# Linear attention feeding a gated MLP: an earlier load of v for batch 4, and another place for relu and minimum of phi(q) in one output stage

## Chip, cores and metric

The kernel runs on one core of a Trainium2 chip. The metric is device time of one launch, in microseconds (us). Of three runs of the kernel before, the median is 271.7 us (271.31 to 272.31).

## What is computed

The reference, cut to what matters (B = 8 batches, 8 heads, S = 576 tokens, head size 64):

```python
phi = lambda x: np.where(x > 0, x, np.exp(x) - 1.0) + 1.0
q_p, k_p = phi(q), phi(k)
kv  = einsum('bhsd,bhse->bhde', k_p, v);  z = sum(k_p, axis=2)
x   = einsum('bhsd,bhde->bhse', q_p, kv) / (einsum('bhsd,bhd->bhs', q_p, z) + 1e-6)
x   = x.transpose(0, 2, 1, 3).reshape(4608, 512)
h   = x @ w_in                          # 512 -> 2048
out = (h * sigmoid(beta * h)) @ w_out   # 2048 -> 512, float32
```

phi(x) is computed as min(exp(x), max(x, 0) + 1): an exponential on ScalarE (ACT, tile `e`, L169), "relu", that is max(x, 0) + 1, on VectorE (DVE, tile `r`, L176), and the minimum of both on VectorE (tile `phi_q` or `phi_k`, L182). Each is done in two halves of the heads (`pr` 0 and 1).

## The kernel before, in words

The order of every engine's queue is written out by hand; semaphores for the dependences are put in by the framework. The work runs in blocks b = 0 to 8. Block b is the MLP for 512 tokens of batch b (the 64 "odd" tokens of each batch that are left over are kept in `xT_tail` and make up block 8). A block has two stages. The H stage computes h = x @ w_in and the gate into `g` (for b = 1 in `h_phase`, for later blocks in `h_fast`, where part of the products is saved by sums and differences of blocks of x and w). The Y stage, `y_fast`, computes the product with w_out by seven products of half size.

In Y the order on TensorE (PE) is: `ya`, `yd` with the sums 2, `ya` again, `yc`, `yb`, then `yd` again with g and `yb` again. Between them VectorE computes u2 = yc + r1 (L1118) and u3 = yd + u2 (L1119), then y2's right half from yb and u3 (L1128), y2's left half from the second yd and u2 (L1131), and y1's right half from the second yb and u2 (L1139). The second `yd` accumulates into the same PSUM bank that u3 reads, so it waits for u3.

Attention for later batches is woven into these stages through two tables, `sh` for H and `sy` for Y: `at(sy, 3, f)` appends f to the list that `run(side, 3)` calls at that place of the stage (L1111 to L1149 show the places of Y: place 2 stands ahead of `yc` and the u sums, place 3 behind them, place 4 behind y2's right half). While block b is computed, batch n = b + 1 has its kv product (`kv_both`, L231, reading `phi_k` and `vaug`) and its numerator (`numer_all`, L344, reading the transposed `qTd`), and batch m = b + 2 has its phi(q) and phi(k). phi(q) is transposed by two DMAs of the SP queue (`q_trans_dma`, L281) into `qTd`.

v of a batch is loaded as float32 into the one tile `vf` (`load_v`, L99, a DMA from the POOL queue) and cast from there to `vaug` (`v_copy`): for batch 3 by ScalarE at place 0 of Y of block 1 (L247), for batches 4 to 7 by GpSimd (POOL, L249) in `next_cast` at place 7 of H. `next_cast` first runs a small copy (`gate`, L1163) that reads what VectorE last wrote, so that the cast starts late enough. Likewise `next_loads(b)` runs a small copy (`gate`, L1156) that reads the end of `qTd` of batch b, so that the loads of v, q and k behind it in the POOL queue start only when the transposes of phi(q) have landed. `tail_copy` (L379) copies the odd tokens of a batch out of `xT` into `xT_tail`, on POOL.

After the H stage's numerator, VectorE forms sums and differences of `g` in `stage` (L831 the differences, L835 to L837 the sums; all bf16, two inputs in SBUF) for the Y stage.

Of the kernel before, what the change touches and what calls it, by code (L numbers as in the profile page):

```python
# [16 lines left out]
def kernel(  # L17
# [12 lines left out]
    B, H, S, D = q.shape  # L30
# [67 lines left out]
    def load(eng, dst, src, b, i0=0, n=4):  # L98
        return eng.dma_start(  # L99
            out=dst.rearrange("p i j d -> p i (j d)"),  # L100
            in_=src[b].rearrange("(i a) (g j) d -> (a g) i (j d)", a=2, j=J)[:, i0 : i0 + n],
        )
# [58 lines left out]
    def table(func):  # L161
        nc.scalar.activation(act0, ones, func)  # L162
# [4 lines left out]
    def phi_exp(b, a, pr, x):  # L167
        e = work.tile([P, 2, J, D], BF16, tag="e", name="e", bufs=4)
        nc.scalar.activation(e, x, ACTF.Exp)  # L169
        st[b, a, pr, "e"] = e  # L170

    def phi_relu(b, a, pr, x):
        if pr == 0:
            st[b, a, "r"] = work.tile([P, 2, 2, J, D], BF16, tag="r", name="r")
        r = st[b, a, pr, "r"] = st[b, a, "r"][:, pr]
        nc.vector.tensor_scalar(r, x, 0.0, 1.0, ALU.max, ALU.add)  # L176

    def phi_tile(b, a):
        st[b, a] = work.tile([P, 2, J, P], BF16, tag=f"phi{a}", name=f"phi_{a}", bufs=1)

    def phi_min(b, a, pr):
        nc.vector.tensor_tensor(  # L182
            st[b, a][:, pr].rearrange("p j (h d) -> p j h d", h=2),
            st[b, a, pr, "e"].rearrange("p h j d -> p j h d"),
            st[b, a, pr, "r"].rearrange("p h j d -> p j h d"),
            ALU.min,
        )

    def xin(b, a, pr):
        if b == 0:  # L190
            return x0f[pr if a == "q" else 2 + pr]
        return (xk if a == "k" else xq)[b % 2][:, 2 * pr : 2 * pr + 2]

    def phi_part(b, a, pr):
        x = xin(b, a, pr)
        phi_exp(b, a, pr, x)
        phi_relu(b, a, pr, x)
        phi_min(b, a, pr)
# [11 lines left out]
    def v_copy(eng, b, pr):  # L210

        copy(
            eng, vaug[b % 2][:, pr, :, :, 0:D],
            (v0b if b == 1 else vf)[:, 2 * pr : 2 * pr + 2].rearrange("p h j d -> p j h d"),
        )
# [5 lines left out]
    def kv_both(b):  # L221

        t = banks("kvp")
        for pr in range(2):
            for j in range(J):
                for il in range(2):
                    for a in range(2):  # L230
                        nc.tensor.matmul(  # L231
                            t[half(il), a, pr * EA : (pr + 1) * EA],
                            st[b, "k"][half(a), pr, j, il * D : (il + 1) * D],
                            vaug[b % 2][half(a), pr, j, il, 0:EA],
                            start=(j == 0), stop=(j == J - 1), skip_group_check=True,
                        )
        tv = t[:, :, 0 : 2 * EA].rearrange("p a (r e) -> p a r e", r=2)
        if b > 1:
            nc.vector.tensor_copy(kv_q[b % 2], tv)
            return  # L240
        st[b, "kv"] = kv_bd.rearrange("p a r h e -> p a r (h e)")
        for il in range(2):
            copy((nc.scalar, nc.vector)[il], kv_bd[half(il), :, :, il], tv[half(il)])
# [34 lines left out]
    def q_trans_dma(b):  # L278
        st[b, "qTd"] = work.tile([P, 2, 2 * J, G], BF16, tag="qT", name="qTd", bufs=1)
        for hh in range(2):  # L280
            nc.sync.dma_start_transpose(  # L281
                out=st[b, "qTd"][:, hh],
                in_=st[b, "q"][half(hh)].rearrange("p a j c -> p (a j c)"),
            )
# [93 lines left out]
    def tail_copy(b):  # L378
        nc.gpsimd.tensor_copy(  # L379
            xT_tail[:, :, b].rearrange("p i r n -> p i (r n)"), xT[b % 2][:, :, 8]  # L380
        )
# [17 lines left out]
    def x_trans_dma(b, t=NT - 1):  # L399
        for pr in range(2):  # L400
            nc.sync.dma_start_transpose(
                out=xT_tail[:, :, b, pr],
                in_=st[b, "xs", t][: rows_of(t), pr * HM : (pr + 1) * HM],
            )
# [64 lines left out]
    def load_qk(b):  # L469
        if b < B:  # L470
            load(nc.gpsimd, xq[b % 2], q, b)
            load(nc.gpsimd, xk[b % 2], k, b)

    def load_v(b):
        if b < B:
            load(nc.gpsimd, v0b if b == 1 else vf, v, b)
# [4 lines left out]
    def w_sum(k, ns=range(2)):  # L481

        for n in ns:
            r = slice(4 * n, 4 * n + 4)
            a, b = (
                (wq(n, HM), wq(n, 0)),
                (wq(2 + n, HM), ws[0][:, r]),
                (wq(2 + n, HM), wq(n, HM)),
                (wq(2 + n, 0), ws[1][:, r]),
            )[k]  # L490
            nc.vector.tensor_sub(ws[k][:, r], a, b)
# [334 lines left out]
    def at(side, n, *fs):  # L826
        side.setdefault(n, []).extend(fs)
# [54 lines left out]
    def h_x_sums(b):  # L882

        t = [h_xs[:, k] for k in range(4)]
        x = lambda r, t: h_x_plain(b, r, t)

        def like(a, c):
            return a.rearrange("p i (t n) -> p i t n", n=c.shape[-1])

        for k, (u, w) in enumerate((  # L890
            (x(0, 1), x(0, 0)), (x(1, 1), t[0]), (x(1, 1), x(0, 1)), (x(1, 0), t[1])
        )):
            nc.vector.tensor_sub(like(t[k], u), u, like(w, u) if k % 2 else w)
# [257 lines left out]
    def next_loads(b):  # L1151

        for pr in range(2) if b == 2 else ():
            v_copy(nc.gpsimd, b, pr)
        if b + 1 < B:
            nc.gpsimd.tensor_copy(gate, st[b, "qTd"][:, 1, 2 * J - 1, G - 1 : G])  # L1156
            load_v(b + 1)
            if b > 2:
                load_qk(b + 1)

    def next_cast(b):

        nc.gpsimd.tensor_copy(gate, gs[2][:, 7, HM - 1 : HM])  # L1163
        for pr in range(2):
            v_copy(nc.gpsimd, b + 1, pr)

    for b in range(1, B + 1):
        n, m = b + 1, b + 2
        sh, sy = {}, {}
        if b == 2 or b == B - 1:  # L1170
            at(sh, 0, lambda: tail_copy(b))
        if n < B:
            at(sh, 0, lambda: next_loads(n))
            if b > 1 and n + 1 < B:
                at(sh, 7, lambda: next_cast(n))
            if b > 2:
                at(sh, 7, lambda: tail_copy(b))
            at(sh, 9 if b == 1 else 0, lambda: kv_both(n))
            at(sh, 12 if b == 1 else 10, lambda: numer_all(n))
        if b == 1:  # L1180
            at(sh, 4, lambda: w_sum(2))
            at(sh, 9, lambda: w_sum(1))
            at(sy, 0, lambda: w_sum(3))
        if m < B:
            at(sy, 0, lambda: phi_tile(m, "q"), lambda: phi_tile(m, "k"))
            if b == 1:

                for pr in range(2):
                    at(sy, 0, lambda pr=pr: phi_exp(m, "q", pr, xin(m, "q", pr)))
                    at(sy, 2, lambda pr=pr: phi_relu(m, "q", pr, xin(m, "q", pr)))  # L1190
                    at(sy, 3 + pr, lambda pr=pr: phi_min(m, "q", pr))
                for pr in range(2):
                    at(sy, 0, lambda pr=pr: v_copy(nc.scalar, m, pr))
                at(sy, 4, lambda: q_trans_dma(m))
                for pr in range(2):
                    at(sy, 5, lambda pr=pr: phi_exp(m, "k", pr, xin(m, "k", pr)))
                    at(sy, 5, lambda pr=pr: phi_relu(m, "k", pr, xin(m, "k", pr)))
                at(sy, 6, lambda: h_x_sums(n))
                for pr in range(2):
                    at(sy, 6, lambda pr=pr: phi_min(m, "k", pr))  # L1200
                at(sy, 6, lambda: table(ACTF.Silu), lambda: x_trans_dma(1, NT - 1))
            else:
                at(sy, 0, lambda: phi_part(m, "q", 0))
                at(sy, 1, lambda: phi_part(m, "q", 1))
                at(sy, 1, lambda: q_trans_dma(m))
                at(sy, 4, lambda: phi_part(m, "k", 0))
                at(sy, 4, lambda: phi_part(m, "k", 1), lambda: table(ACTF.Silu))
        if b == B - 2:
            at(sy, 0, lambda: h_w_sums(2))
        if 2 <= b < B:  # L1210
            at(sy, {B - 2: 4, B - 1: 0}.get(b, 6), lambda: h_x_sums(n))
        (h_phase if b < 2 else h_fast)(b, xT[b % 2] if b < B else xT_tail, sh)
        y_fast(b, sy)
# [30 lines left out]
```

## Time and profile before

| what | value |
|---|---|
| median of three runs | 271.7 us |
| the profiled execution, its own time | 271.53 us |
| span of its instructions | 269.8 us |
| PE busy in the span | 262.0 us (97%) |
| DVE busy | 211.3 us (78%) |
| ACT busy | 169.0 us (63%) |
| POOL busy | 46.0 us (17%) |
| TensorE clock granted | 1.0 |

Times below are microseconds from the start of the span. In a timeline a row has the start, the time from the start to the end of the merged instructions, the engine, the line, the operation, what it writes and reads, the count, and in brackets how long the engine had been idle and on what. Starts of successive PE rows tell more than their ends, which overlap: two products of 16 matmuls stand 1.75 us apart when PE does not wait. Y of block 1 runs from 64.77 to about 77.3, H of block 2 to 92.5, Y of block 2 from 92.53 to about 105.7.

### The profile page before, as it was taken

The page shows a single profiled execution, that of the slowest core. Times are in us where ns is not written, and L with a number is a line of the kernel's source. Part 1 is how long each engine was busy: PE and PEld are TensorE (multiplying, and loading weights), DVE is VectorE, ACT ScalarE, POOL GpSimd, SP SyncE. Part 2 cuts the span into 40 slices and gives each one's busy share as a digit, 9 for nine tenths or more (in the row PEclk, how much of TensorE's full clock was granted, in tenths as well). Part 3 has the DMA queues.
Part 4 walks back from the last instruction along what each step waited for, and adds up shares of the span by engine and source line. Part 5 has one row for each costly group of instructions (what it writes and reads, how often), then busy time and mean ns, then how long its engine had stood idle before and what let it go on. Part 6 is the DMA issues. An engine that isn't in the chain of part 4 may idle for free.

```text
span 269.8 us, 6793 instructions
## 1 busy us (share of the span) xinstructions
PE 262.0 (97%) x2846; PEld 182.1 (68%) x2851; DVE 211.3 (78%) x412; ACT 169.0 (63%) x241; POOL 46.0 (17%) x72
## 2 busy tenths in 40 slices
PE   7899999999999998999999999999999999999994
PEld 3584455446866586658864886588658866886793
DVE  4853697998995999689968986899689667856862
ACT  4958885987954993499449944894483048415810
POOL 5842305121003300340034003300000000000000
PEclk9999999999999999999999999999999999999999
DMA  7999999999349997998599979995504050023013
GB/s 235 242 206 286 303 326 239 299 212 260 74 78 229 245 145 104 277 217 90 90 255 243 99 92 248 242 108 87 158 2 88 4 156 2 0 64 94 0 41 117
DMA packets 49262, 42.19 MB, mean 156 GB/s; under 512 B 30400, under 2 KB 41296, under 8 KB 49232
## 3 DMA queue, kind: packets, MB, share of 16 engines
q0 software_dynamic: 13344, 22.81, 37.6%
q1 hardware_dynamic: 35568, 18.75, 35.4%
q8 instruction: 22, 0.36, 0.5%
q10 hardware_dynamic: 320, 0.20, 0.3%
q14 instruction: 8, 0.07, 0.1%
HBM read 36.71 MB, written 9.44 MB: 171 GB/s over the span
## 4 chain that ended last, share of the span: by engine, by line
PE 61%; DVE 1%; issue 0%; DVEq 0%
PE h_ps L413 21%; PE yd L1095 8%; PE ya L1095 8%; PE yb L1095 7%; PE hc L902 5%; PE hz L902 4%; PE yc L1095 4%; PE yb L1067 1%; PE kvp L231 1%; PE nps L344 1%; DVE phi_q L182 1%; DVE u L1119 0%; DVE u L1118 0%; DVE r L176 0%; DVE y L1075 0%
## 5 line engine op out<-in xcount | busy, mean ns | idle before, releaser
L421 ACT ACTIVATE g<-h_ps,beta_c 128x512 bf16<-128x512 f32 x108 | 71.5, 692 | 60.7 <-PE h_ps L413 60.1
L413 PE MATMUL h_ps<-xT,w_in 128*128 128x512 bf16 (+2 forms) x424 | 94.8, 367 | 0.0
L413 PEld LDWEIGHTS <-w_in 128*128 128x128 bf16 x456 | 42.8, 98 | 37.9
L1095 PEld LDWEIGHTS <-stage 128*128 128x128 bf16 x480 | 46.9, 98 | 5.6 <-DVE stage L831 0.2
L1095 PEld LDWEIGHTS <-g 128*128 128x128 bf16 x384 | 37.5, 98 | 7.2 <-issue 1.2
L1095 PE MATMUL ya<-w_out,g 128*128 128x256 bf16 x256 | 30.6, 273 | 0.0
L359 DVE TENSOR_TENSOR xs_sb<-nps,rden 128x448 bf16<-128x448 f32 (+2 forms) x24 | 18.2, 758 | 0.8
L169 ACT ACTIVATE e<-xk 128x1152 bf16<-128x1152 bf16 (+1 forms) x15 | 16.7, 1159 | 0.4 <-DMA xk<-in_k_dram 0.4
L1095 PE MATMUL yd<-ws,g 128*128 128x256 bf16 x128 | 15.3, 272 | 0.9 <-DVE u L1119 0.9
L962 ACT ACTIVATE g<-hc,beta_c 128x512 bf16<-128x512 f32 x18 | 11.4, 683 | 7.3 <-DVE hc L948 7.3
L169 ACT ACTIVATE e<-xq 128x1152 bf16<-128x1152 bf16 x14 | 15.6, 1159 | 0.0
L162 ACT ACT_TABLE_LOAD x12 | 15.4, 1283 | 0.2
L1095 PE MATMUL yd<-ws,stage 128*128 128x256 bf16 x128 | 15.3, 273 | 0.0
L1095 PE MATMUL yc<-ws,stage 128*128 128x256 bf16 x128 | 15.3, 273 | 0.0
L428 PE MATMUL y_ps<-w_out,g 128*128 128x512 bf16 x60 | 14.8, 379 | 0.2
L182 DVE TENSOR_TENSOR phi_q<-e,r 128x1152 bf16<-128x1152 bf16 x16 | 12.3, 767 | 2.2 <-ACT e L169 1.2
L902 PEld LDWEIGHTS <-w_in 128*128 128x128 bf16 x108 | 10.5, 98 | 4.9
L182 DVE TENSOR_TENSOR phi_k<-e,r 128x1152 bf16<-128x1152 bf16 x16 | 12.7, 803 | 1.2
L902 PEld LDWEIGHTS <-h_w 128*128 128x128 bf16 x112 | 11.0, 98 | 3.8
L1095 PE MATMUL yb<-ws,stage 128*128 128x256 bf16 x112 | 13.4, 273 | 0.0
L1095 PE MATMUL yb<-w_out,stage 128*128 128x256 bf16 x112 | 13.4, 273 | 0.0
L962 ACT ACTIVATE g<-c,beta_c 128x512 bf16<-128x512 f32 x18 | 12.3, 727 | 0.9 <-DVE c L945 0.9
(146 smaller groups left out, 375.3 us busy)
## 6 DMA issues: line engine op xcount, KB each, us to landing
out_dram<-y SPq DMA_DIRECT2D x29, 256.0 KB, 3.8
vf<-in_v_dram POOLq DMA_DIRECT2D x6, 1152.0 KB, 9.3
xq<-in_q_dram POOLq DMA_DIRECT2D x7, 576.0 KB, 13.6
xk<-in_k_dram POOLq DMA_DIRECT2D x7, 576.0 KB, 15.7
g<-in_moe_w_out_dram POOLq DMA_DIRECT2D x2, 1024.0 KB, 17.7
stage<-in_moe_w_out_dram POOLq DMA_DIRECT2D x4, 512.0 KB, 17.6
w_in<-in_moe_w_in_dram POOLq DMA_DIRECT2D x3, 512.0 KB, 12.7
stage<-in_q_dram SPq DMA_DIRECT2D x2, 576.0 KB, 4.4
```

The source lines that it names most:

```text
L162: nc.scalar.activation(act0, ones, func)
L169: nc.scalar.activation(e, x, ACTF.Exp)
L182: nc.vector.tensor_tensor(st[b, a][:, pr].rearrange("p j (h d) -> p j h d", h=2), st[b, a, pr, "e"].rearrange("p h j d -> p j h d"), st[b, ...
L231: nc.tensor.matmul(t[half(il), a, pr * EA : (pr + 1) * EA], st[b, "k"][half(a), pr, j, il * D : (il + 1) * D], vaug[b % 2][half(a), pr, j, ...
L344: nc.tensor.matmul(ps[half(n), v % 7 * EA : (v % 7 + 1) * EA], st[b, "qTd"][half(il), a, pr * J + j, :], kv_q[b % 2][half(il), a, pr, :], ...
L359: nc.vector.tensor_mul(xs_sb[:, ils, v0 * D : v1 * D].rearrange("p i (u d) -> p i u d", d=D), pv[:, :, :, 0:D], rden[:, :, :, None].to_bro ...
L413: nc.tensor.matmul(hp[:, c0:c1].rearrange("p (t n) -> p t n", n=n), w_in_sb[ff // 4][:, kc, (ff % 4) * P : (ff % 4 + 1) * P], xm, start=(f ...
L421: nc.scalar.activation(g_sb[b % 2][:, ff, :], hp, ACTF.Silu, scale=beta_c[:, ff : ff + 1])
L428: nc.tensor.matmul(yp[:, c0:c1], g_sb[b % 2][:, ff, t * P : (t + 1) * P], w_out_sb[i][:, c, c0:c1], start=(ff == 0), stop=(ff == FC - 1), ...
L902: nc.tensor.matmul(o, lhs[:, i, a * P : (a + 1) * P], m, start=(first and a == 0 and i == 0), stop=True, skip_group_check=True,)
L962: nc.scalar.activation(g_sb[b % 2][:, ff].rearrange("p (t n) -> p t n", t=2), src, ACTF.Silu, scale=beta_c[:, ff : ff + 1],)
L1095: nc.tensor.matmul(ps[:, p * HM : (p + 1) * HM], lhs(c, p), rhs(c), start=(first and p == 0 and c == 0), stop=True, skip_group_check=True,)
```

## The change

In H of block 2 (`next_loads(3)`) the load of v of batch 4 is put ahead of the gate on `qTd` of batch 3; q and k of batch 4 stay behind it. `tail_copy(2)` is put behind these loads; it stood ahead of all of them. So POOL's order there goes from tail copy, gate, v, q, k to v, gate, q, k, tail copy.

In Y of block 1 both relus of q (batch 3) go from place 2 to place 3, and the minimum of half 0 from place 3 to place 4, where that of half 1 stood. So DVE's order there goes from relu, relu, u2, u3, min, y2 right, min, y2 left to u2, u3, relu, relu, y2 right, min, min, y2 left. The two transposes of phi(q) stay behind the second minimum.

```diff
@@ next_loads(b)
         if b + 1 < B:
+            if b == 3:
+                load_v(b + 1)
             nc.gpsimd.tensor_copy(gate, st[b, "qTd"][:, 1, 2 * J - 1, G - 1 : G])
-            load_v(b + 1)
+            if b != 3:
+                load_v(b + 1)
             if b > 2:
                 load_qk(b + 1)
@@ the loop over blocks
-        if b == 2 or b == B - 1:
+        if b == B - 1:
             at(sh, 0, lambda: tail_copy(b))
         if n < B:
             at(sh, 0, lambda: next_loads(n))
+            if b == 2:
+                at(sh, 0, lambda: tail_copy(b))
...
                 for pr in range(2):
                     at(sy, 0, lambda pr=pr: phi_exp(m, "q", pr, xin(m, "q", pr)))
-                    at(sy, 2, lambda pr=pr: phi_relu(m, "q", pr, xin(m, "q", pr)))
-                    at(sy, 3 + pr, lambda pr=pr: phi_min(m, "q", pr))
+                    at(sy, 3, lambda pr=pr: phi_relu(m, "q", pr, xin(m, "q", pr)))
+                    at(sy, 4, lambda pr=pr: phi_min(m, "q", pr))
```

## The prediction

> **What bounds the kernel now.** I read the engines' shares first, then the chain of waits in order of time, then the timelines of PE, DVE and POOL around its start.
>
> ```profile
> PE 262.0 (97%) x2846; PEld 182.1 (68%) x2851; DVE 211.3 (78%) x412; ACT 169.0 (63%) x241; POOL 46.0 (17%) x72
> ```
>
> PE is busy for 97% of the span, so there is little to win. The chain in order of time tells where PE still waits:
>
> ```profile
> 100.83 0.61 DVE u L1118
> 101.45 0.02 issue
> 101.47 0.70 DVE u L1119
> 102.17 0.04 issue
> 102.21 1.91 PE yd L1095 x16
> 104.12 1.75 PE yb L1095 x16
> ```
>
> From 102.21 to 265.98 every piece of the chain is PE, with no gap. What ends PE's last wait is u3 of Y of block 2 (L1119). Whatever makes PE arrive earlier at 102.21 makes the kernel shorter by as much; nothing behind it can add a gain. So I list PE's gaps ahead of it, in the stretch that the change touches (73 to 102), from its timeline:
>
> ```profile
> 71.75 1.91 PE L1095 MATMUL yb<-ws,stage 128*128 128x256 bf16 x16
> 73.83 1.91 PE L1095 MATMUL yd<-ws,g 128*128 128x256 bf16 x16 [0.17 <-DVE u L1119]
> ...
> 80.35 1.03 PE L413 MATMUL h_ps<-xT,w_in 128*128 128x512 bf16 x4
> 81.31 0.89 PE L231 MATMUL kvp<-vaug,phi_k 64*64 64x65 bf16 x72
> ...
> 99.58 1.91 PE L1095 MATMUL yb<-ws,stage 128*128 128x256 bf16 x16
> 102.21 1.91 PE L1095 MATMUL yd<-ws,g 128*128 128x256 bf16 x16 [0.73 <-DVE u L1119]
> ```
>
> A product takes 1.75 from start to start. So `yd` of block 1 could start at 71.75 + 1.75 = 73.50 and starts at 73.83: **0.33 lost**. `yd` of block 2 could start at 101.33 and starts at 102.21: **0.88 lost**. Four h_ps matmuls take 0.86 in the chain, so `kvp` (batch 3) could start at 81.21 and starts at 81.31: 0.10 lost, to the minimum of phi_k. All other starts of these 28 us follow one another within 0.1. The three gaps make 1.31, the most that this change can give.
>
> Now what holds DVE ahead of u3 in each Y stage:
>
> ```profile
> 71.63 0.82 DVE L176 TENSOR_SCALAR r<-xq 128x1152 bf16<-128x1152 bf16 x2
> 72.37 0.68 DVE L1118 TENSOR_TENSOR u<-yc,r 128x512 f32<-128x512 f32 x1
> 73.09 0.69 DVE L1119 TENSOR_TENSOR u<-yd,u 128x512 f32<-128x512 f32 x1
> ...
> 92.79 1.48 DVE L831 TENSOR_TENSOR stage<-g 128x1024 bf16<-128x1024 bf16 x1
> ```
>
> In block 1 the two relus stand in front of u2, although yc had ended at 71.75 + 0.16 = 71.91. In block 2 DVE is busy without a pause from the numerator (88.34) to 102.16, and one difference of g, at 92.79, takes 1.48. The same one in block 3 takes 0.68. POOL's rows show what stands beside it:
>
> ```profile
> 91.49 2.23 POOL L249 CAST vaug<-vf 128x1152 bf16<-128x1152 f32 x2 [2.66 <-DMA vf<-in_v_dram]
> 108.25 0.19 POOL L1156 COPY gate<-qTd 128x1 bf16<-128x1 bf16 x1 [14.52 <-DMA qTd<-phi_q]
> ...
> 116.68 2.23 POOL L249 CAST vaug<-vf 128x1152 bf16<-128x1152 f32 x2 [0.79 <-PE nps L344]
> ```
>
> In block 2 the two casts of v of batch 4 run from 91.49 to 93.72, because POOL had waited 2.66 for the load; the difference starts inside and ends 0.55 behind them. A minimum of phi_k (54.61) also took 1.51, against 0.76 for its twin at 56.59, beside POOL's casts of batch 2 (53.05 to 55.51). In block 3 the casts (116.68 to 118.91) stand beside evacuations that read PSUM, which keep their times (L359 at 116.63 takes 0.62, as it does at 88.77 with POOL idle).
>
> The Trainium skill, "SBUF — State Buffer", section "Who interferes with whom", has a rule for this: a VectorE instruction with two SBUF inputs contends with a GpSimd one that reads SBUF, and the one that comes second is fully blocked. By that rule the difference was held by the second cast and the evacuations are safe; the trace agrees with both (1.48 and 0.62). By a rule that spared two-input instructions the 1.48 would have another cause and the cast part below would be worth 0 instead of 0.80.
>
> **The change part by part.**
>
> *The u sums ahead of the relus (Y of block 1).* u2 now waits for yc: in blocks 3 and 4 it starts 0.04 behind yc's end (128.02, 155.44), so here at 71.95. u3 follows 0.72 later at 72.67 and ends at 73.36. `yd` started 0.05 behind u3, so 73.41 is open to it, ahead of 73.50: the gap of 0.33 goes. But DVE's work of this stage is only reordered, and the next thing that PE takes from it is the minimum of phi_k, for `kvp`. I walk DVE with the start-to-start steps of before (relu 0.37, a sum 0.60, minimum behind minimum 0.66): relus 73.28 and 73.65, y2 right 74.02 (yb has ended at 73.66), minima 74.62 and 75.28, y2 left 75.94, relus of k 76.54 and 76.91, y1 right 77.28 (its yb has ended at 77.16), the four sums of x from 77.88, minima of k from 79.34, the last ends at 80.76. Before it ended at 81.01. So DVE gains 0.25: it loses 0.32 to the new wait for yc, and saves 0.16 ahead of y2 left and 0.32 ahead of y1 right, where it had waited for PE. `kvp` started 0.30 behind that minimum: 81.06 or 81.07, while PE would be there at 81.21 - 0.33 = 80.88. **Gain 0.24**; the other 0.09 turns into a longer wait ahead of `kvp`. Bounds: 0.43 if `kvp` were not to wait (0.33 + 0.10), and -0.32 if DVE got nothing back for its wait on yc. I take 0.24, the walk, since every step has a row.
>
> The second minimum ends at 76.03 instead of 75.71, so the transposes of phi(q) start 0.32 later in SP's queue, and the four y stores behind them too. The stores' tiles are written next in Y of block 2 (102.25). `qTd` is read by the numerator at 87.88 and had landed by 82.10, when the gate ran: 5 us of cover.
>
> *v of batch 4.* `vf` is one tile, and its last reader is the cast of batch 3 on ACT (69.66 to 71.85). The load is issued about 72.1 instead of 82.67. Three loads of v took 6.4 to 8.7 to land: 78.5 to 80.8. The cast then waits only for the gate behind the difference of g (88.64 + 0.19), and runs from about 88.9 to 91.1, beside evacuations from PSUM. The difference starts at 92.55 on the shifted clock, 1.4 behind the casts, and takes 0.68: DVE gains 1.48 - 0.68 = 0.80, all in front of u2 and u3. Check: u2 of block 2 would start at 100.75 - 0.80 = 99.95, behind yc (99.58 + 0.16 + 0.04 = 99.78), so DVE still sets it; u3 ends at 101.36, `yd` starts 0.05 behind, 0.08 after 101.33. **Gain 0.80** of the 0.88; bounds 0 and 0.88.
>
> The load moved past the gate meets an idle stretch: the DMA share is 0.01 from 72 to 76. POOL has nothing else to issue before the gate. q and k of batch 4 are issued behind the gate as before, without v in front of them: v took 0.76 of issue and 1152 KB. The exponential of k waited 0.17 for its load at 98.79; that wait should go, and is off the path. If this cover were gone, and q late, relu of q at 98.30 would wait.
>
> *The tail copy* (0.40, 0.88 where it met a minimum) goes from 73.82 to about 84.5. POOL's next work is the gate at 88.64, and the DVE sums beside it (83.64, 84.44) read PSUM: nothing. Its new wait behind it, the transpose into the same xT, comes at 119.77.
>
> **Sum:** 0.24 + 0.80 = 1.04. The profiled execution took 271.53 (span 269.8 and 1.73 around it), so 270.49; on the median of the runs, 0.17 higher, 270.66. I say **270.6**.
>
> **Rivals.**
> 1. *Only the cast counts.* If the walk through Y of block 1 is 0.25 too hopeful, PE waits for `kvp` until 81.31 as before and 0.80 is left: 270.73. For it: DVE is full there (3.90 of 4.00 from 72 to 76).
> 2. *Only the relus count.* The difference at 92.79 stays slow, because v lands late or its delay has another cause: 271.53 - 0.24 = 271.29, on the median 271.46. Against it: the two slow rows, both beside casts.
> 3. *All gaps close*, if DVE's steps pack tighter than the rows: 271.53 - 1.31 = 270.22, from the lowest run 270.0.
> 4. *Slower.* v of batch 4 (1152 KB) now stands in front of the two transposes of phi(q) of batch 3. They are started at 76.2 and took 6.2 to land. The numerator needs them by 87.88 - 0.24 = 87.64, so this decides from a delay of 87.64 - 82.10 - 0.32 = 5.2 us. If v landed after 19.5, the longest of its loads, at 91.6, and the transposes only behind it, at 97.8, PE would wait about 10.2: 271.53 + 10.2 - 0.24 = 281.5. Against it: 19.5 is from the full queues of the kernel's start; here the DMA engines are idle, and 8.7 is the most seen near.
>
> **How the numbers follow.** Half a per cent, 1.36 us, is about what a measurement of this kernel can tell from no change. Forecast 0.58, rival 1 0.13, rival 2 0.14, rival 3 0.09, rival 4 0.06. The forecast and rivals 1 to 3 lie within half a per cent, since even all gaps are 1.31; the runs spread over 1.0, so I give 0.08 to faster by more, from the forecast's lower edge and rival 3. Slower by more is rival 4: 0.06. Same: 0.86. The range goes from rival 3 (270.0) to rival 2 (271.5).
>
> **What would show it.** In the profile after: the load of v at about 72; POOL's casts from about 88.9; the difference at about 92.5 with 0.68; u3 of block 1 ahead of the end of `yb`; `yd` 1.75 behind `yb` in block 1, and within 0.1 of that in block 2; `kvp` about 0.2 behind its h_ps. Wrong it would be if a two-input DVE instruction falls under the moved casts, if the gate on `qTd` runs after 87, or if PE gets gaps behind 102.

## The result and the profile after

The changed kernel takes 270.54 us (median of 9 runs, 269.93 to 270.73) where the kernel before took 271.53 (9 runs, 271.05 to 272.31): a ratio of 0.9962, with a 95% interval of 0.995 to 0.9975. That is about 1.0 us, inside half a per cent. The profiled execution took 270.39 with a span of 268.6 (before 271.53 and 269.8).

The engines' busy time in the profile after, from the page; it answers to the line of before that the prediction opens with:

```profile
PE 262.8 (98%) x2851; PEld 182.4 (68%) x2851; DVE 209.7 (78%) x412; ACT 169.0 (63%) x241; POOL 45.9 (17%) x72
```

The shares hardly move, as they must for 0.4%. (The line of before has 2846 matmuls to 2851 weight loads; five matmul records are missing there.) What moved is seen in PE's timeline at the three gaps:

```profile
71.76 1.91 PE L1095 MATMUL yb<-ws,stage 128*128 128x256 bf16 x16
73.50 1.91 PE L1095 MATMUL yd<-ws,g 128*128 128x256 bf16 x16
...
80.03 1.03 PE L413 MATMUL h_ps<-xT,w_in 128*128 128x512 bf16 x4
80.98 0.93 PE L231 MATMUL kvp<-vaug,phi_k 64*64 64x65 bf16 x72
...
99.33 1.91 PE L1095 MATMUL yb<-ws,stage 128*128 128x256 bf16 x16
101.13 1.91 PE L1095 MATMUL yd<-ws,g 128*128 128x256 bf16 x16
```

`yd` of block 1 now stands 1.74 behind `yb` (2.08 before), `yd` of block 2 stands 1.80 behind (2.63 before), and the brackets that named u3 as the releaser are gone. DVE's and POOL's rows that answer to those of before:

```profile
72.03 0.69 DVE L1118 TENSOR_TENSOR u<-yc,r 128x512 f32<-128x512 f32 x1 [0.41 <-PE yc L1095]
72.75 0.69 DVE L1119 TENSOR_TENSOR u<-yd,u 128x512 f32<-128x512 f32 x1
73.36 0.82 DVE L176 TENSOR_SCALAR r<-xq 128x1152 bf16<-128x1152 bf16 x2
...
92.51 0.68 DVE L831 TENSOR_TENSOR stage<-g 128x1024 bf16<-128x1024 bf16 x1
```

```profile
72.15 0.76 POOL L99 DMA_DIRECT2D vf<-in_v_dram  x1 [9.66 <-ACT vaug L247]
82.52 0.19 POOL L1158 COPY gate<-qTd 128x1 bf16<-128x1 bf16 x1 [9.61 <-DMA qTd<-phi_q]
...
88.48 2.23 POOL L249 CAST vaug<-vf 128x1152 bf16<-128x1152 f32 x2
```

u2 waits for yc instead of standing behind the relus. The load of v is issued at 72.15, when ACT has cast batch 3. POOL's casts run from 88.48 to 90.71 without a wait for a DMA, and the difference of g at 92.51 meets nobody: 0.68 instead of 1.48.

For what follows, one measure is freer of noise than the whole time: the stretch from the start of `yb` of block 1 to the start of the second `yd` of block 2. The start of `yb` itself wanders by 0.6 us from execution to execution (71.66 to 72.26 over all profiles), by work that the change doesn't touch, and behind that `yd` every profile but one (told below) has 167.4 to 167.7 us to the end of its span. The stretch is not free of noise either: there is one profile of each kernel, the two of the changed kernel differ by 0.13, and the 72 small matmuls of `kvp` and of the numerator take 0.73 to 0.86 each from profile to profile.

| kernel | stretch, us | median, us | ratio to before, 95% |
|---|---|---|---|
| before | 30.46 | 271.53 | 1 |
| changed | 29.37 | 270.54 | 0.9962 (0.995 to 0.9975) |
| relus only | 30.84 | 271.91 | 1.0012 (0.9997 to 1.0028) |
| load only | 29.64 | 270.79 | 0.9979 (0.9967 to 0.9991) |
| before without the casts of v of batch 4 | 29.57 | 270.57 | 0.9968 (0.9956 to 0.9981) |
| changed, casts held back | 30.90 | 272.13 | 1.0024 (1.0012 to 1.0036) |
| relus only, without the casts | 29.24 | 270.17 | 0.9953 (0.994 to 0.9966) |
| changed, tail copy ahead | 29.35 | 270.47 | 0.9962 (0.995 to 0.9974) |
| changed, q and k ahead too | 29.40 | 270.76 | 0.9973 (0.9964 to 0.9983) |
| changed, u first in Y of block 2 too | 29.16 | 270.96 | 0.9979 (0.9968 to 0.9991) |
| changed, once more | 29.24 | 270.52 | 0.9958 (0.9944 to 0.9973) |
| changed, u first in block 2, v of batch 5 ahead | 29.20 | 270.50 | 0.9961 (0.9947 to 0.9974) |

### The profile page after: what moved, and what is told of

Its sections match the earlier page's. It is cut to its first block, busy times and chain, and to the rows that moved or that the text cites. A ratio compares the mean times of both kernels' runs of the same rounds, so it can differ in the third digit from the quotient of the medians.

```text
span 268.6 us, 6799 instructions
## 1 busy us (share of the span) xinstructions
PE 262.8 (98%) x2851; PEld 182.4 (68%) x2851; DVE 209.7 (78%) x412; ACT 169.0 (63%) x241; POOL 45.9 (17%) x72
## 4 chain that ended last, share of the span: by engine, by line
PE 95%; DMA 2%; ACT 1%; DVE 1%; SPq 0%; issue 0%
PE h_ps L413 35%; PE yd L1095 10%; PE ya L1095 10%; PE yb L1095 9%; PE hc L902 6%; PE y_ps L428 5%; PE yc L1095 5%; PE hz L902 4%; PE kvp L231 2%; DMA stage<-in_q_dram 2%; PE nps L344 2%; PE yb L1067 1%; ACT e L169 1%; PE nps L309 1%; PE kvp L566 0%; PE xtp L393 0%
## 5 line engine op out<-in xcount | busy, mean ns | idle before, releaser
L428 PE MATMUL y_ps<-w_out,g 128*128 128x512 bf16 x64 | 15.4, 379 | 0.0
```

The costliest lines, as they stand in the source:

```text
L428: nc.tensor.matmul(yp[:, c0:c1], g_sb[b % 2][:, ff, t * P : (t + 1) * P], w_out_sb[i][:, c, c0:c1], start=(ff == 0), stop=(ff == FC - 1), ...
```

## The experiments

**The two parts alone.** First only the moves in Y of block 1, with `next_loads` and `tail_copy` as before:

```diff
-                    at(sy, 2, lambda pr=pr: phi_relu(m, "q", pr, xin(m, "q", pr)))
-                    at(sy, 3 + pr, lambda pr=pr: phi_min(m, "q", pr))
+                    at(sy, 3, lambda pr=pr: phi_relu(m, "q", pr, xin(m, "q", pr)))
+                    at(sy, 4, lambda pr=pr: phi_min(m, "q", pr))
```

> Only the relus and minima of q move in Y of block 1; the loads stay as before. Theory (two separate gains): yd of block 1 starts 1.75 behind yb (73.50) instead of 2.08; everything up to the numerator of block 2 is 0.25 to 0.3 earlier; the difference of g in block 2 (L831, second half) keeps its 1.48 and the gap ahead of yd of block 2 its 0.9. Time 0.25 to 0.35 us below before (ratio about 0.999). Rival (the gain of block 1 is eaten by the wait for phi_k's minimum): kvp of block 2 at 81.3 as before, ratio 1.000. Second rival (the cast follows the relus, not the load): the whole 1.0 us.

Measured: 271.91, ratio 1.0012 (0.9997 to 1.0028). The theory's 0.999 lies outside that interval, and the rivals' reasons are not in the trace either: `yd` of block 1 does start 1.75 behind `yb`, and the numerator of block 2 is earlier, yet the stretch is 0.38 longer than before. (The interval reaches to 0.9997, so the times alone say no gain, and leave open whether it is a loss.) DVE's timeline of this run has two slow instructions in block 2 where the kernel before had one:

```profile
92.64 1.25 DVE L831 TENSOR_TENSOR stage<-g 128x1024 bf16<-128x1024 bf16 x1
93.81 1.63 DVE L835 TENSOR_TENSOR stage<-g 128x1024 bf16<-128x1024 bf16 x1
```

and POOL's timeline tells where they come from:

```profile
82.72 0.19 POOL L1156 COPY gate<-qTd 128x1 bf16<-128x1 bf16 x1 [8.11 <-DMA qTd<-phi_q]
83.29 0.75 POOL L99 DMA_DIRECT2D vf<-in_v_dram  x1 [0.38 <-issue]
...
92.20 2.69 POOL L249 CAST vaug<-vf 128x1152 bf16<-128x1152 f32 x2 [3.52 <-DMA vf<-in_v_dram]
```

The second minimum of phi(q) ends later, so do the transposes, the gate (82.72, before 82.10), the load (83.29, before 82.67) and the casts (92.20, before 91.49), while PE and DVE are earlier. This execution is 0.18 late as a whole by the start of its `yb` (71.93, before 71.75); behind that start the gate and the load are 0.44 later and the casts 0.53. The casts now hold the difference and the sum behind it; together they lose about 1.5 instead of 0.80. `yd` of block 2 waits 1.27 for u3 and stands 1.43 later than PE could have started it (0.88 before); 0.22 more is lost inside `yc`, since `yb` stands 1.97 behind it.

Then only the load ahead of the gate (with the tail copy behind), the relus as before:

```diff
+            if b == 3:
+                load_v(b + 1)
             nc.gpsimd.tensor_copy(gate, st[b, "qTd"][:, 1, 2 * J - 1, G - 1 : G])
-            load_v(b + 1)
+            if b != 3:
+                load_v(b + 1)
```

> Only the load of v of batch 4 goes ahead of the gate (and the tail copy behind); the relus stay in front of u2. Theory: the 0.33 gap ahead of yd of block 1 stays, POOL's casts end by 91.2, the difference in block 2 takes 0.68, yd of block 2 starts within 0.1 of 1.75 behind yb. Time 0.75 to 0.9 us below before (ratio 0.997). Rival (both parts are needed together, since DVE's lateness comes from Y of block 1): under 0.4 us.

Measured: 270.79, ratio 0.9979 (0.9967 to 0.9991), the stretch 0.82 shorter. The difference takes 0.68, the gap ahead of `yd` of block 1 stays (74.14 - 72.08 - 1.75 = 0.31), that of block 2 falls to 0.14, not quite to the 0.1 of the theory. The trace bears the theory out. The times are weaker: they give about 0.6 where 0.75 to 0.9 was expected, and their interval (0.24 to 0.9 us) doesn't rule out the rival's 0.4; the stretch of 0.82 speaks against it. So the parts don't add: the relus give nothing alone, and with the load they give the rest.

**Is it the cast, or the landing of the load?** In the kernel before, the casts follow at once on the landing, so its trace can't tell them apart. This kernel is the one before without POOL's casts of batch 4:

```diff
-        for pr in range(2):
+        for pr in range(2) if b != 3 else ():
             v_copy(nc.gpsimd, b + 1, pr)
```

> The kernel before without POOL's two casts of v of batch 4 (that batch is computed with the v that stands in the buffer from batch 2); the load keeps its place and lands at 91.4 as before. Theory (the cast holds VectorE): the difference takes 0.68, the gap ahead of yd of block 2 falls from 0.88 to under 0.1, time 0.75 to 0.9 us below before, as with the early load. Rival (the landing of the load, or DMA traffic, slows the difference): it keeps 1.48 and the time stays that of before.

Measured: 270.57, ratio 0.9968 (0.9956 to 0.9981), the stretch 0.89 shorter. DVE's row of the difference:

```profile
92.75 0.68 DVE L831 TENSOR_TENSOR stage<-g 128x1024 bf16<-128x1024 bf16 x1
```

The load keeps its place (82.84) and lands 8.5 later, at 91.3, as before; the gap ahead of `yd` of block 2 falls from 0.88 to 0.14. It is the cast. The counterpart is the changed kernel, its load early, with the casts held back until the numerator is written:

```diff
-        nc.gpsimd.tensor_copy(gate, gs[2][:, 7, HM - 1 : HM])
+        last = xs_sb[:, 1, 18 * D - 1 : 18 * D] if b == 3 else gs[2][:, 7, HM - 1 : HM]
+        nc.gpsimd.tensor_copy(gate, last)
...
-            if b > 1 and n + 1 < B:
+            if b > 2 and n + 1 < B:
                 at(sh, 7, lambda: next_cast(n))
...
             at(sh, 12 if b == 1 else 10, lambda: numer_all(n))
+            if b == 2:
+                at(sh, 10, lambda: next_cast(n))
```

> The changed kernel, its load still early, but POOL's casts of v of batch 4 are held until VectorE has written the last rows of the numerator of batch 3, so they fall beside the differences and sums of g (two inputs in SBUF each). Theory: each cast holds VectorE once, by 0.5 to 1.1 us; the gap ahead of yd of block 2 opens to 0.6 to 2.1 us; time 0.6 to 2.1 above the changed kernel (271.1 to 272.6). Rival (the place of the load is what matters, not that of the cast): 270.5 as the changed kernel.

Measured: 272.13, ratio 1.0024 (1.0012 to 1.0036); 1.6 above the changed kernel, the stretch 1.53 longer. DVE's timeline and POOL's:

```profile
92.94 0.69 DVE L835 TENSOR_TENSOR stage<-g 128x1024 bf16<-128x1024 bf16 x1
93.67 1.51 DVE L836 TENSOR_TENSOR stage<-stage,g 128x1024 bf16<-128x1024 bf16 x1
95.22 1.52 DVE L837 TENSOR_TENSOR stage<-g,stage 128x1024 bf16<-128x1024 bf16 x1
```

```profile
92.91 0.19 POOL L1167 COPY gate<-xs_sb 128x1 bf16<-128x1 bf16 x1 [7.89 <-DVE xs_sb L359]
93.03 3.16 POOL L249 CAST vaug<-vf 128x1152 bf16<-128x1152 f32 x2
```

Two casts, two sums held, by 0.82 and 0.83. PE loses 1.38 by it ahead of `yd` of block 2 (a gap of 1.43 where the changed kernel has 0.05) and 0.37 at `yc`, which waits for a late sum (3.86 from the `ya` ahead of it to `yb`, 3.49 in the changed kernel). POOL pays too: its two casts take 3.16 where they take 2.23 beside the evacuations. The Trainium skill, "SBUF — State Buffer", section "SBUF: two separate sides", says that whichever instruction comes first holds the shared pair of ports for its whole length and the other fully blocks; the trace agrees with it in that both sides lose, 0.82 and 0.83 on VectorE and 0.93 on GpSimd.

**Where the gain of the relus went.** The relus only, as in the first experiment, and POOL's casts of batch 4 left out with the edit of the third:

> The relus moved, the loads as before, and POOL's casts of v of batch 4 left out (that batch is computed with the v that stands in the buffer from batch 2). The relus alone gave 1.0012 of before: in its trace PE gained 0.15 to 0.25 up to the numerator, but the transposes of phi(q) started 0.4 later, the load behind the gate 0.6 later, and the casts (92.20 to 94.89) held two DVE instructions instead of one. New theory (the gain of the relus is real and is lost again only through the gate, the load and the later casts): without the casts the relus give 0.2 to 0.35 on top of the run without casts, so 270.2 to 270.4, 1.0 to 1.2 below before. Rival (the relus give nothing of their own): 270.57, as the run without casts alone.

Measured: 270.17, ratio 0.9953 (0.994 to 0.9966), the stretch 29.24. Against the run without casts alone (29.57) the relus give 0.33; in medians 0.40. The rival (nothing of their own) falls. With the early load the relus give 29.64 - 29.37 = 0.27 by the first profile of the changed kernel and 0.40 by the second (29.24, told below).

**What the moved tail copy and the gate do.** The changed kernel with the tail copy of batch 2 ahead again:

```diff
-        if b == B - 1:
+        if b == 2 or b == B - 1:
             at(sh, 0, lambda: tail_copy(b))
...
-            if b == 2:
-                at(sh, 0, lambda: tail_copy(b))
```

> The changed kernel with the tail copy of batch 2 where it stood, ahead of the loads. It waits for its transposes until about 73.9, so the load of v is issued at about 74.7 instead of 72.15 and lands at about 81, still ahead of the gate at 88.4. Theory (8 us of cover): 270.5 as the changed kernel; the copy takes 0.5 to 0.9 instead of 0.42 where it meets DVE. Rival (the tail copy's place carries part of the gain, by delaying the load into the transposes): 0.2 us or more slower, with qTd landing later than 82.5.

Measured: 270.47, ratio 0.9962 (0.995 to 0.9974), the stretch 29.35. The load is issued at 74.72, 2.6 later, the gate runs at 83.24 instead of 82.52, and the casts still start at 88.80 without a wait. The transposes were slowed a little, as the rival said (6.65 from their issue to the gate instead of 6.26), but nobody waits for that: the tail copy's place is worth nothing.

The changed kernel with q and k of batch 4 ahead of the gate as well:

```diff
             if b == 3:
                 load_v(b + 1)
+                load_qk(b + 1)
             nc.gpsimd.tensor_copy(gate, st[b, "qTd"][:, 1, 2 * J - 1, G - 1 : G])
...
-            if b > 2:
+            if b > 3:
                 load_qk(b + 1)
```

> The changed kernel with q and k of batch 4 ahead of the gate as well, so that three loads stand in front of the transposes of phi(q) (prediction's fourth rival, with three times its load). Theory (the DMA engines are shared, so these loads take from the transposes): qTd lands between 84 and 90 instead of 82.5; PE waits ahead of the numerator of block 2 only if that is later than 87.6; time 270.5 if it is earlier, up to 2.5 us more if later. Rival (transposes pass the loads untouched): qTd at 82.5 and 270.5.

Measured: 270.76, ratio 0.9973 (0.9964 to 0.9983), some 0.2 above the changed kernel, which the times alone can't tell from it. POOL's row of the gate in this run, where `qTd` lands:

```profile
88.06 0.19 POOL L1159 COPY gate<-qTd 128x1 bf16<-128x1 bf16 x1 [13.09 <-DMA qTd<-phi_q]
```

The transposes land 5.5 later than in the changed kernel (88.06 against 82.52), though they start only 0.5 later (76.75), and PE waits for them ahead of the numerator: it starts 1.55 behind the six h_ps ahead of it (87.99 - 86.44), where it is 1.39 in the changed kernel (87.59 - 86.20). In all other profiles this step is 1.38 or 1.39. This is the prediction's fourth rival at work, at 0.16 us: it does decide from 5 us of delay, and v alone doesn't bring one.

**One step further.** The changed kernel with the second half of phi(q) and its transposes behind the u sums in Y of block 2 too:

```diff
-                at(sy, 1, lambda: phi_part(m, "q", 1))
-                at(sy, 1, lambda: q_trans_dma(m))
+                at(sy, 3 if b == 2 else 1, lambda: phi_part(m, "q", 1))
+                at(sy, 3 if b == 2 else 1, lambda: q_trans_dma(m))
```

> The changed kernel with the second half of phi(q) and its transposes behind the u sums in Y of block 2 too. Theory: the 0.05 that is left ahead of yd of block 2 goes, 0.05 below the changed kernel at most, less than these rounds tell apart: 270.5. Rival (the transposes of phi(q) of batch 4 then start some 0.1 to 0.8 later, and with them the gate, the load and the casts of batch 5, which fall into the differences of block 3, as the relus alone did in block 2): 0.3 to 1 us slower.

Measured: 270.96, ratio 0.9979 (0.9968 to 0.9991). The rival held in kind: the stretch falls to 29.16, and block 3 gives more back. Its size was off: DVE now waits 0.93 for `yc`, and the transposes start at 102.67, 2.3 later behind `yb` of block 1 than in the changed kernel (99.90), not 0.1 to 0.8. POOL's and DVE's rows of block 3:

```profile
118.70 2.23 POOL L249 CAST vaug<-vf 128x1152 bf16<-128x1152 f32 x2 [3.44 <-PE h_ps L413]
```

```profile
120.03 1.46 DVE L831 TENSOR_TENSOR stage<-g 128x1024 bf16<-128x1024 bf16 x1
121.41 0.88 DVE L835 TENSOR_TENSOR stage<-g 128x1024 bf16<-128x1024 bf16 x1
```

The casts of batch 5 start at 118.70 instead of 115.72 (116.49 in the second profile of the changed kernel) and fall into the differences of block 3; `yd` there stands 2.43 behind `yb` (127.19, 129.62). This is the one profile with 168.3 instead of 167.4 to 167.7 behind the stretch. (The row names h_ps as what ended POOL's wait. The load of v of batch 5 was issued at 109.58 and took 9.0 to land, at 118.6, so the cast waited for the load.) The mend is the change's own: on top of the edit above, v of batch 5 ahead of its gate, run beside the changed kernel once more.

```diff
-            if b == 3:
+            if b in (3, 4):
                 load_v(b + 1)
...
-            if b != 3:
+            if b not in (3, 4):
                 load_v(b + 1)
```

> The changed kernel once more, beside the next. 270.5, ratio 0.996; from yb of block 1 to the second yd of block 2 29.35 to 29.45 us, from there to the end of the span 167.5.

> The u sums first in Y of block 2 too, and v of batch 5 loaded ahead of its gate as v of batch 4 is (it can start when POOL has cast batch 4, at about 91). u first alone shortened the stretch from yb of block 1 to the second yd of block 2 to 29.16 from 29.37, but lost 0.8 in block 3, where the casts of batch 5 came 2.6 later and met the differences. Theory: with the early load these casts start behind their gate at about 115 and meet nothing; the stretch stays 29.16, from there to the end 167.5; 0.2 below the changed kernel, 270.3. Rival (v of batch 5 lands in the transposes or takes from the loads of q and k of batch 4): the transposes of batch 3's x or q and k land late and 0.2 or more is lost.

Measured: the changed kernel 270.52 (ratio 0.9958, 0.9944 to 0.9973), this one 270.50 (0.9961, 0.9947 to 0.9974). The casts of batch 5 start at 114.86 and meet nothing, and what they cost in block 3 is gone, but the 0.2 that was expected is not there: the stretches are 29.24 and 29.20, which is within what two profiles of the changed kernel differ by, and behind the stretch this kernel has 167.72 where the changed kernel has 167.47 and 167.43. PE's rows at the start of block 3 show 0.15 of that:

```profile
106.27 1.04 PE L413 MATMUL h_ps<-xT,w_in 128*128 128x512 bf16 x4
107.29 0.61 PE L902 MATMUL hz<-xs_sb,h_w 128*128 128x256 bf16 x4
```

The four h_ps take 1.02 from start to start, 0.87 in both profiles of the changed kernel. The first hz reads the sums of x (L893). DVE makes them later here, since it has waited 0.92 for `yc` ahead of u2: the second of them ends at 107.23, 0.06 ahead of hz, where it ended at 106.41 in the changed kernel. So u first in block 2 closes a gap of 0.05 to 0.14 and opens one of 0.15. There is no better version here that these runs can tell apart; PE has next to no gaps left in this stretch.

## Why the prediction held, and where it did not

The time (270.6 forecast, 270.54 measured), the sign and the place within half a per cent came out. By its steps:

- *PE's gaps, and nothing to gain behind 102.* Right: behind `yd` of block 2 the profiles before and after are alike (167.6 and 167.5 to the span's end). One small gap was passed over: the first `yd` of block 2 stood 1.80 behind `ya` (92.53, 94.33), since it reads the slow difference; after, 1.75. And the third gap, 0.10 ahead of `kvp`, is none: `kvp` stands 0.95 or 0.96 behind its four h_ps in all 12 profiles, though the minimum of phi_k had ended 0.30 ahead of it before and 0.13 after, and in block 3 of before it is the same 0.96 (105.70, 106.66). So the most to win was 1.21 by the prediction's list, not 1.31.
- *The u sums first.* Forecast 0.24, measured 0.27 to 0.40 wherever the casts are out of the way. DVE's walk was right to 0.1 at every row (u2 72.03 for 71.95, y2 left 76.03 for 75.94, last minimum of phi_k's end 80.85 for 80.76). (The prediction names 0.16 and 0.32 as what DVE saves and 0.32 as what it loses, which is 0.16 and not 0.25; the walk is right, because y1 right had started 0.40 later than its steps allow, of which 0.32 stood in its bracket.) The mis-sized term is the wait ahead of `kvp`: it was to start 0.30 behind that minimum, a step taken from one row of before, and starts 0.13 behind it. The 0.30 was slack, since `kvp` had not waited for the minimum; so the 0.09 that were to be lost there were not lost, and `kvp` is earlier by the whole 0.34 (9.22 behind `yb` of block 1, 9.56 before). That the changed kernel comes so close to the 0.24 is in part luck: in its profile `kvp` and the numerator take 0.04 and 0.10 longer than before, which the prediction didn't foresee, and PE begins Y of block 2 only 0.20 earlier.
- *The early load.* Forecast 0.80, measured 0.82 (load alone) and 0.89 (casts taken out). That the cast and not the load held the difference was argued from two rows; leaving it out and holding it back have shown it. The load landed after 5.9 us, a little sooner than the 6.4 to 8.7 taken.
- *The later transposes.* Their 0.32 was costed at nothing, with the numerator as the only reader, and in the changed kernel that holds (gate 82.52, numerator 87.59). But the gate reads them too, and with the load still behind the gate the same 0.32 moves the casts. So rival 2's price for the relus alone, 0.24 below before, was wrong: they give a ratio of 1.0012. The prediction treated two gains as separate that are not; in the kernel that was asked about, the load's move is what makes the relus' gain safe.
- *The tail copy* at nothing: shown. *Rival 4*: its mechanism is there, and one load is too little for it.

## What to carry to other kernels

When an engine's step is moved later, follow every queue that hangs on it, gates included, not only the reader of its data: a delay with 5 us of cover at one reader had none at another. A change that looks worth a few tenths may be worth nothing alone and its full amount beside another, when it moves work into a window that the other clears; so test the parts and the whole. A GpSimd cast of 1.14 us that met VectorE instructions with two SBUF inputs cost VectorE up to 0.95 us here (0.80 in the kernel before, 0.82 and 0.83 with the casts held back), and where a DMA's landing decides when the cast starts, a small delay elsewhere decides whether it meets one. And a row that starts a little behind another need not have waited for it: `kvp` kept its 0.95 behind the matmuls ahead of it, however early the minimum of phi_k ended.

## What the runs showed of the hardware

The spread was not expected. Runs whose casts of one batch start on a DMA's landing near the differences scatter widely: standard deviation 0.40 to 0.54 us for before (four sets of 9 to 31 runs), 0.37 for the relus only, 0.42 for u first in block 2. Where the casts are left out, held until VectorE has written a result, or early, they scatter by 0.13 to 0.25: 0.15 and 0.17 without the casts, 0.14 with the casts held back (slow, but always by the same), 0.17 with the load alone, 0.25 and 0.23 for the changed kernel. In the set of 31, the fastest run of before takes 270.37, as little as the changed kernel, while the 12 runs of the relus only stay above 271.3. With 5 to 12 runs in most sets the step from 0.25 to 0.37 is small. That the cast's start is what scatters is concluded from this grouping; the start itself was seen only in the one profile of each kernel.
